# The low parts of g move from VectorE to GpSimd while the second layer's weights are prepared

## The chip, the cores and the metric

The kernel runs on one core of one Trainium2 chip. A core has a matrix engine (TensorE: PE in the views, with its weight loads as PEld), a vector engine (VectorE: DVE), an activation engine (ScalarE: ACT), a general engine (GpSimd: POOL) and a queue that issues transfers (SyncE: SP). Each works through its own instructions in order and waits on semaphores for the others. The metric is the device time of one execution in microseconds (us); lower is better.

## The reference, cut to what is computed

```python
def reference(x, state, moe_w_gate, moe_w1, moe_w2, moe_capacity, moe2_w_in, moe2_w_out):
    a = attention(x, state)                  # 4 x 8 x (512 + 32) x 64, softmax both ways
    t = a.transpose(0, 2, 1, 3).reshape(2176, 512)
    t = moe(t, moe_w_gate, moe_w1, moe_w2, moe_capacity)   # 8 experts, best one per row
    return _moe2_ref(t, moe2_w_in, moe2_w_out)

def _moe2_ref(x, w_in, w_out):               # w_in 512 x 2048, w_out 2048 x 512
    h = x @ w_in
    relu6 = np.clip(h + 3.0, 0.0, 6.0)
    g = h * relu6 / 6.0
    return (g @ w_out).astype(np.float32)
```

The inputs of this last function, the "second layer" here, are 64-bit floats in its weights and 32-bit floats in its rows.

## The kernel before

The first 262 us of the profiled execution are attention and the experts; their result lies as rows in `y_pad`. What the change touches is the second layer that follows. Its rows are taken in seven chunks of 256, and its inner width of 2048 in 16 slices of 128, numbered m. For one slice and one chunk the work is this:

- `mm3` (line 1100) computes 128 columns of h for the 256 rows on TensorE, in twelve matmuls (line 1109): each operand is kept as a high and a low part in a reduced float format (`yTh`, `yTl` of the rows, `wh`, `wl` of the weights), and high by high, high by low and low by high are summed. The eight with `wh` come first, the four with `wl` last. Then ScalarE makes `u` (line 1121), VectorE makes `g` (line 1122, one operand in SBUF and one in PSUM), ScalarE rounds it to the high part `gh` (line 1123), and line 1124 subtracts for the low part `gl`. `u` and `g` have two buffers each, `gh` and `gl` seven.
- `mm4` (line 1127) multiplies `gh` and `gl` by the slice's rows of `w_out`, in six matmuls (line 1132), and adds into two PSUM banks; the third of the six is the first to read `gl`.

The weights are made ready on the way. `vload` (line 921) fetches a slice's 64-bit weights in two loads of 512 KB by SP; `vconv` (line 930) turns each load into 32-bit floats with three VectorE instructions (lines 937, 939, 941), and `advance(NA)` issues the next two of them. `prep(m)` (line 945) has ScalarE round the slice to `wh` (line 955) and GpSimd subtract for `wl` (line 956, 128 x 1024). This is needed once, so it goes on beside the first group of two chunks, `gi == 0`; the five chunks after it find all weights ready.

One step of the first group, for a slice m from 1 to 15, is issued in this order: `mm3(m)` of chunk 0, two conversion instructions, `mm3(m)` of chunk 1, two conversion instructions, `prep(m + 2)`, and then `mm4(m - 1)` of both chunks. So TensorE has 24 matmuls of line 1109 and then 24 of line 1132 in a step. VectorE has in a row: g, gl, two conversions, g, gl, two conversions. ScalarE has u, gh, u, gh, wh. GpSimd has one `wl`, and nothing else until the first results are stored (line 1253). The 51 conversion instructions that are left at slice 1 run out in step 13. The order is the program's own; nothing is rearranged.

After the chunks stands a general loop (lines 1351 to 1367) for inputs that fill an expert unevenly; it doesn't run here, and it calls `mm3` without the new argument.

Of the kernel before, what the change touches and what calls it, by code (L numbers as in the profile page):

```python
# [7 lines left out]
F32 = mybir.dt.float32  # L8
# [4 lines left out]
ALU = mybir.AluOpType  # L13
# [582 lines left out]
def full(ctx, tc, x, state, w_gate, w1, w2, capacity, w_in, w_out, out, dbg=None):  # L596
    nc = tc.nc
    V, A, G, T = nc.vector, nc.scalar, nc.gpsimd, nc.tensor
# [316 lines left out]
    def fetch_c(c):  # L915
        return fetch(lambda t: slice(256 * c + 128 * t, 256 * c + 128 * t + 128), c % 3)
# [28 lines left out]
    def prep(m):  # L945
        v = vt.pop(m).bitcast(F32)
        if m == 0:
            wh = vv.tile([128, 1024], F32R, name="wh0")
            wl = vv.tile([128, 1024], F32R, name="wl0")
        elif m < 3:  # L950
            wh, wl = (rw.tile([128, 1024], F32R, name=f"w{n}{m}", tag="raw0") for n in "hl")
        else:
            wh = vv.tile([128, 1024], F32R, name=f"wh{m}", tag=f"v{m - NV - 1}") if m > NV else mw.tile([128, 1024], F32R, name=f"wh{m}")
            wl = mw.tile([128, 1024], F32R, name=f"wl{m}")
        A.copy(wh, v)  # L955
        (V if m in (0, 2) else G).tensor_tensor(out=wl, in0=v, in1=wh.bitcast(F32), op=ALU.subtract)  # L956
        WM[m] = (wh, wl)
# [3 lines left out]
    def advance(n):  # L961

        while n and nextv[1] < 32:
            if nextv[2] is None:
                while nextv[0] < min(32, nextv[1] + NL2):
                    vload(nextv[0])
                    nextv[0] += 1
                nextv[2] = vconv(nextv[1])
            if next(nextv[2], 0) == 0:
                nextv[1] += 1  # L970
                nextv[2] = None
            n -= 1
# [124 lines left out]

    turn3 = [0]

    def mm3(m, yTh, yTl, early=False):  # L1100
        wh, wl = WM[m]
        turn3[0] ^= 1
        ps = (p3.tile([128, 256], F32, name="p3", tag="3") if turn3[0] else pT.tile([128, 256], F32, name="p3", tag="T"))
        pv = ps.rearrange("p (t j) -> p t j", t=2)
        n = 0
        for ops in (((wh, yTh), (wh, yTl)), ((wl, yTh),)):
            for k in range(4):
                for l, r in ops:
                    T.matmul(pv, l[:, 128 * k:128 * k + 128], r[:, :, 128 * k:128 * k + 128], start=n == 0, stop=n == 11)  # L1109
                    n += 1  # L1110
        if early:
            ug = ew.tile([128, 2, ROW], F32, name="xg", bufs=3)
            u, g = ug[:, 0, 0:256], ug[:, 1, 0:256]
            ghl = mk.tile([128, YR], F32, name="yg").bitcast(F32R)
            gh, gl = ghl[:, 0:256], ghl[:, 256:512]
        else:
            u = mw.tile([128, 256], F32, name="u", bufs=2)
            g = mw.tile([128, 256], F32, name="g", bufs=2)
            gh = mw.tile([128, 256], F32R, name="gh", bufs=NH)
            gl = mw.tile([128, 256], F32R, name="gl", bufs=NH)  # L1120
        A.activation(out=u, in_=ps, func=AF.Relu, bias=b3)  # L1121
        V.scalar_tensor_tensor(out=g, in0=u, scalar=6.0, in1=ps, op0=ALU.min, op1=ALU.mult)  # L1122
        A.copy(gh, g)  # L1123
        V.tensor_tensor(out=gl, in0=g, in1=gh.bitcast(F32), op=ALU.subtract)  # L1124
        return gh, gl

    def mm4(m, gh, gl, po, ts=(0, 1)):
        wh, wl = WM[m]
        for t in ts:
            ls = slice(128 * t, 128 * t + 128)  # L1130
            for i, (l, r) in enumerate(((gh, wh), (gh, wl), (gl, wh))):
                T.matmul(po[t], l[:, ls], r[:, 512:1024], start=m == 0 and i == 0, stop=m == 15 and i == 2)  # L1132

    def accs():
        return [pM.tile([128, 512], F32, name="po", tag="M") for _ in range(2)]
# [23 lines left out]
    ft, pr, pe, pg, pid, pth, py = {}, {}, {}, {}, {}, {}, {}  # L1159
# [16 lines left out]
    for s in range(N0, NF):  # L1176
# [59 lines left out]
        if pend and pend[0][0] == s + 2:  # L1236
            p_begin()
    g0 = mm3(0, *ft[0][0][0:2], True)
    g1 = mm3(0, *ft[1][0][0:2], True)
    po = {c: accs() for c in (0, 1)}  # L1240
    late = (0, (0, 1), {0: g0, 1: g1}, po)
# [5 lines left out]
    def put(po, fid, t):  # L1247
        o = mw.tile([128, DM], F32, name="o", bufs=4)
        if t:
            V.tensor_scalar(out=o, in0=po[t], scalar1=C6, scalar2=None, op0=ALU.mult)  # L1250
        else:
            A.activation(out=o, in_=po[t], func=AF.Copy, scale=C6)  # L1252
        G.indirect_dma_start(out=out, out_offset=bass.IndirectOffsetOnAxis(ap=fid[:, t:t + 1], axis=0), in_=o, in_offset=None,  # L1253
                             bounds_check=B * (S + NS) - 1, oob_is_err=False)

    groups = [(0, 1)] + [(c,) for c in range(2, NCS)]
    for gi, gs in enumerate(groups):
        last = gi + 1 == len(groups)
        if gi:
            po = {}  # L1260
        held = {}
        for m in range(0 if gi else 1, 16):
            if gi == 0 and m in (2, 4, 6):
                r = slice(3 * m - 6, min(3 * m, 17))
                nc.sync.dma_start(out=out.rearrange("(p r) d -> p r d", r=17)[:, r], in_=zt[:, 0:DM].unsqueeze(1).broadcast_to([128, r.stop - r.start, DM]))
            gg = {}
            for c in gs:
                gg[c] = mm3(m, *ft[c][0][0:2])
                if gi == 0:
                    advance(NA)  # L1270
            if gi == 0 and m + 2 < 16:
                prep(m + 2)
            lm, ls, lg, lpo = late
            for c in ls:
                if c == NCS - 1 and lm >= 16 - NH:

                    held[lm] = lg[c]
                    mm4(lm, *lg[c], lpo[c], (0,))
                    continue
                mm4(lm, *lg[c], lpo[c])  # L1280
                if lm == 15:
                    put(lpo[c], ft[c][0][2], 0)
                    put(lpo[c], ft[c][0][2], 1)
            if m == 0:
                for c in gs:
                    po[c] = accs()
            late = (m, gs, gg, po)
            if not last and m >= 10:
                for c in groups[gi + 1]:
                    if m == 10:  # L1290
                        ft[c] = fetch_c(c)
                    if m in (12, 14):
                        ft[c][1](m // 2 - 6)
# [104 lines left out]
```

## Time and profile before

| what | us |
|---|---|
| median of three runs | 594.09 (591.84 to 594.51) |
| the profiled execution | 592.67 |
| its span, first to last instruction | 590.9 |
| steps 3 to 15 of the second layer's first group | 276.77 to 358.52 |

TensorE is busy 95% of the span, VectorE 53%, ScalarE 38%, GpSimd 20%. These are averages over stages with different limits. The page's strip of 40 slices shows the busy share of each engine in tenths; VectorE stands at 5 to 8 between 260 and 350 us and at 3 to 4 after it, while TensorE stands at 9 nearly throughout. The granted TensorE clock is full in all slices of the second layer. A row of a timeline gives the start, the duration, the engine, the line and the operation, and in brackets the idle time before it with what ended it. A duration counts from the moment the instruction has what it waited for by semaphore, so a time in which it then can't proceed is inside it.

### The profile page before, as it was taken

To read this page: it belongs to the slowest core of one execution; us is meant where nothing else is said; L and a number is where in the kernel's file an instruction comes from. 1 tells how busy PE (TensorE), PEld (TensorE's weight loads), DVE (VectorE), ACT (ScalarE), POOL (GpSimd) and SP (SyncE) were. 2 spreads that over 40 slices of the span, in tenths; PEclk is the share of its full clock that TensorE was granted. 3 is DMA by queue.
4 is the path that set the end of the run, shared out by engine and by line. 5 is a ranking of instruction groups with operands and counts; after the bars stand their busy time and mean duration, and the time that the engine had idled before them with its cause. 6 is when DMAs were issued, how large, how long until landed. Compare 5 with 4: busy or idle time off the path is not lost.

```text
span 590.9 us, 10478 instructions
## 1 busy us (share of the span) xinstructions
PE 559.8 (95%) x3974; PEld 483.8 (82%) x3974; DVE 316.0 (53%) x726; ACT 222.1 (38%) x462; POOL 118.8 (20%) x169
## 2 busy tenths in 40 slices
PE   6998899899999999999998989999999999999996
PEld 3655689786968798899987768999999999999995
DVE  5788885364726555366888874234334334234331
ACT  4877631242304150325334334233233333333331
POOL 4436534210600110013334431100001001000001
PEclk9999699799999999999999999999999999999999
DMA  6745612998869783244863411001001001000000
GB/s 140 169 161 174 230 76 59 319 361 297 309 216 391 226 312 109 95 136 129 295 201 109 142 55 53 37 2 55 18 1 55 19 0 55 19 1 18 19 2 29
DMA packets 52201, 75.26 MB, mean 127 GB/s; under 512 B 23121, under 2 KB 31313, under 8 KB 51634
## 3 DMA queue, kind: packets, MB, share of 16 engines
q1 hardware_dynamic: 49634, 67.09, 34.1%
q0 software_dynamic: 2240, 7.38, 3.8%
q8 instruction: 33, 0.54, 0.4%
q14 instruction: 22, 0.18, 0.1%
q10 hardware_dynamic: 272, 0.07, 0.0%
HBM read 70.75 MB, written 16.49 MB: 148 GB/s over the span
## 4 chain that ended last, share of the span: by engine, by line
issue 35%; PE 26%; DVE 11%; DMA 6%; ACT 3%; POOL 1%; POOLq 0%; ACTq 0%; DVEq 0%
PE pm L807 9%; PE pm L796 5%; DMA out_dram<-o,fid 5%; PE p L1109 3%; DVE v L941 3%; PE po L1132 3%; PE pm L1064 2%; PE pm L1084 2%; DVE gl L1124 2%; DVE v L939 2%; DVE v L937 2%; DMA st<-in_moe_w_in_dram 2%; ACT w2h L743 1%; ACT gh L1123 1%; DVE g L1122 1%
## 5 line engine op out<-in xcount | busy, mean ns | idle before, releaser
L1109 PE MATMUL p<-yTh,wh 128*128 128x256 f32 x448 | 110.6, 280 | 0.5 <-ACT wh L955 0.5
L1109 PE MATMUL p<-yTl,wh 128*128 128x256 f32 x448 | 110.5, 280 | 0.0
L1122 DVE SCALAR_TENSOR_TENSOR g<-u,p 128x256 f32<-128x256 f32 x110 | 46.1, 419 | 109.3 <-ACT u L1121 109.3
L1121 ACT ACTIVATE u<-p,b 128x256 f32<-128x256 f32 x110 | 52.1, 474 | 106.8 <-PE p L1109 106.7
L1109 PEld LDWEIGHTS p<-yTh,wh 128*128 128x128 f32 x448 | 84.4, 188 | 4.8 <-ACT wh L955 1.0
L1109 PEld LDWEIGHTS p<-yTl,wh 128*128 128x128 f32 x448 | 84.5, 189 | 3.9
L1132 PE MATMUL po<-wh,gh 128*128 128x512 f32 x220 | 86.8, 394 | 0.8 <-ACT gh L1123 0.6
L1132 PE MATMUL po<-wl,gh 128*128 128x512 f32 x220 | 86.1, 391 | 0.0
L1132 PE MATMUL po<-wh,gl 128*128 128x512 f32 x220 | 86.1, 391 | 0.0
L1124 DVE TENSOR_TENSOR gl<-g,gh 128x256 fp32r<-128x256 f32 x110 | 54.2, 493 | 51.9 <-ACT gh L1123 51.9
L1123 ACT CAST gh<-g 128x256 fp32r<-128x256 f32 x110 | 44.7, 406 | 89.6 <-DVE g L1122 89.6
L1109 PE MATMUL p<-yTh,wl 128*128 128x256 f32 x448 | 71.7, 282 | 5.4 <-POOL wl L956 5.4
L1109 PEld LDWEIGHTS p<-yTh,wl 128*128 128x128 f32 x448 | 60.8, 189 | 6.6 <-POOL wl L956 6.6
L1253 POOL DMA_INDIRECT out_dram<-o,fid x14 | 13.8, 988 | 219.5 <-ACT o L1252 162.2
L956 POOL TENSOR_TENSOR wl<-v,wh 128x1024 fp32r<-128x1024 f32 x14 | 35.3, 2523 | 101.4 <-ACT wh L955 83.3
L1132 PEld LDWEIGHTS po<-wh,gl 128*128 128x128 f32 x220 | 41.3, 188 | 10.0 <-DVE gl L1124 0.8
L1132 PEld LDWEIGHTS po<-wh,gh 128*128 128x128 f32 x220 | 41.4, 188 | 7.4 <-ACT gh L1123 2.4
L796 PE MATMUL pm<-xth,w1h 128*128 128x256 f32 x160 | 46.5, 291 | 0.5 <-ACTq L1156 0.5
L796 PE MATMUL pm<-xtl,w1h 128*128 128x256 f32 x160 | 45.7, 286 | 0.0
L796 PE MATMUL pm<-xth,w1l 128*128 128x256 f32 x160 | 45.6, 285 | 0.0
L1132 PEld LDWEIGHTS po<-wl,gh 128*128 128x128 f32 x220 | 41.4, 188 | 5.1
L807 PE MATMUL pm<-htl,w2h 128*128 128x256 f32 x160 | 44.9, 281 | 0.3 <-DVE htl L799 0.2
(284 smaller groups left out, 985.7 us busy)
## 6 DMA issues: line engine op xcount, KB each, us to landing
raw<-in_moe_w_dram SPq DMA_DIRECT2D x80, 512.0 KB
st<-in_moe_w_in_dram SPq DMA_DIRECT2D x16, 512.0 KB
st<-in_moe_w_out_dram SPq DMA_DIRECT2D x16, 512.0 KB
x_rows<-xrow SPq DMA_DIRECT2D x4, 1072.0 KB
xb<-in_x_dram SPq DMA_DIRECT2D x32, 128.0 KB
yg<-y_pad SPq DMA_DIRECT2D x14, 258.0 KB
out_dram<-zt SPq DMA_DIRECT2D x2, 1536.0 KB
y_pad<-y SPq DMA_DIRECT2D x5, 516.0 KB
```

The lines of the kernel that those rows point to most:

```text
L796: T.matmul(ps[:, j], W1[l][k][:, ls], xT[r][:, k], start=k == 0 and i == 0, stop=k == 3 and i == 2)
L807: T.matmul(ps[:, j], W2[l][k // 2][:, k % 2, ls], hT[k // 2][r][:, k % 2], start=k == 0 and i == 0, stop=k == 7 and i == 2)
L937: V.tensor_scalar(out=t, in0=hi, scalar1=3, scalar2=0x3FFFFFFF, op0=ALU.logical_shift_left, op1=ALU.bitwise_and)
L941: V.scalar_tensor_tensor(out=t, in0=lo, scalar=29, in1=t, op0=ALU.logical_shift_right, op1=ALU.bitwise_or)
L956: (V if m in (0, 2) else G).tensor_tensor(out=wl, in0=v, in1=wh.bitcast(F32), op=ALU.subtract)
L1109: T.matmul(pv, l[:, 128 * k:128 * k + 128], r[:, :, 128 * k:128 * k + 128], start=n == 0, stop=n == 11)
L1121: A.activation(out=u, in_=ps, func=AF.Relu, bias=b3)
L1122: V.scalar_tensor_tensor(out=g, in0=u, scalar=6.0, in1=ps, op0=ALU.min, op1=ALU.mult)
L1123: A.copy(gh, g)
L1124: V.tensor_tensor(out=gl, in0=g, in1=gh.bitcast(F32), op=ALU.subtract)
L1132: T.matmul(po[t], l[:, ls], r[:, 512:1024], start=m == 0 and i == 0, stop=m == 15 and i == 2)
L1253: G.indirect_dma_start(out=out, out_offset=bass.IndirectOffsetOnAxis(ap=fid[:, t:t + 1], axis=0), in_=o, in_offset=None, bounds_check=B * ...
```

## The change

`mm3` gets an argument for the engine that makes `gl`, VectorE unless told otherwise. In the first group, slices 1 to 13 name GpSimd: 26 instructions. Slices 14 and 15, slice 0 (made earlier, line 1238) and the other five chunks stay on VectorE.

```diff
-    def mm3(m, yTh, yTl, early=False):
+    def mm3(m, yTh, yTl, early=False, eng=V):
...
-        V.tensor_tensor(out=gl, in0=g, in1=gh.bitcast(F32), op=ALU.subtract)
+        eng.tensor_tensor(out=gl, in0=g, in1=gh.bitcast(F32), op=ALU.subtract)
...
-                gg[c] = mm3(m, *ft[c][0][0:2])
+                gg[c] = mm3(m, *ft[c][0][0:2], eng=V if gi or m > 13 else G)
```

VectorE's instructions of slice 3 and the start of slice 4, before (the number behind a name is the buffer; g_3853 and g_3879 are slice 3 of chunk 0 and 1, st is a loaded weight and v its conversion):

```order
L1122 SCALAR_TENSOR_TENSOR g_3853<-u_3852,p3_3839 128x256
L1124 TENSOR_TENSOR gl_3855<-g_3853,gh_3854 128x256
L941 SCALAR_TENSOR_TENSOR v8_3756<-st_3728,v8_3756 128x512
L937 TENSOR_SCALAR v9_3863<-st_3754 128x512
L1122 SCALAR_TENSOR_TENSOR g_3879<-u_3878,p3_3865 128x256
L1124 TENSOR_TENSOR gl_3881<-g_3879,gh_3880 128x256
L939 SCALAR_TENSOR_TENSOR v9_3863<-st_3754,v9_3863 128x512
L941 SCALAR_TENSOR_TENSOR v9_3863<-st_3754,v9_3863 128x512
L1122 SCALAR_TENSOR_TENSOR g_3919<-u_3918,p3_3905 128x256
```

The same stretch of VectorE now:

```order
L1122 SCALAR_TENSOR_TENSOR g_3853<-u_3852,p3_3839 128x256
L941 SCALAR_TENSOR_TENSOR v8_3756<-st_3728,v8_3756 128x512
L937 TENSOR_SCALAR v9_3863<-st_3754 128x512
L1122 SCALAR_TENSOR_TENSOR g_3879<-u_3878,p3_3865 128x256
L939 SCALAR_TENSOR_TENSOR v9_3863<-st_3754,v9_3863 128x512
L941 SCALAR_TENSOR_TENSOR v9_3863<-st_3754,v9_3863 128x512
L1122 SCALAR_TENSOR_TENSOR g_3919<-u_3918,p3_3905 128x256
```

The two gl are gone, and a g is followed by conversions at once.

GpSimd's instructions of slices 2 to 4 (gl of two chunks each) with the low weights of slices 3 to 6 (wl3 to wl6), as the difference:

```order
 L956 TENSOR_TENSOR wl3_3759<-v3_2733,wh3_3758 128x1024
+L1124 TENSOR_TENSOR gl_3791<-g_3789,gh_3790 128x256
+L1124 TENSOR_TENSOR gl_3814<-g_3812,gh_3813 128x256
 L956 TENSOR_TENSOR wl4_3824<-v4_2993,wh4_3823 128x1024
+L1124 TENSOR_TENSOR gl_3855<-g_3853,gh_3854 128x256
+L1124 TENSOR_TENSOR gl_3881<-g_3879,gh_3880 128x256
 L956 TENSOR_TENSOR wl5_3889<-v5_3282,wh5_3888 128x1024
+L1124 TENSOR_TENSOR gl_3921<-g_3919,gh_3920 128x256
+L1124 TENSOR_TENSOR gl_3946<-g_3944,gh_3945 128x256
 L956 TENSOR_TENSOR wl6_3957<-v6_3469,wh6_3956 128x1024
```

Between two wl now stand the two gl of the slice in work. TensorE, ScalarE and SP have the same rows as before.

## Rows read from the trace of the kernel before

**Rows 1.** Busy us (instructions) by engine, granted clock, DMA, in two stretches
```profile
298.00:358.00 60.00, 53.32 (x327) 45.45 (x327) 48.46 (x75) 24.20 (x50) 22.78 (x9) 1.00 0.39 125
366.00:422.00 56.00, 56.00 (x362) 50.91 (x361) 18.94 (x46) 19.17 (x43) 4.98 (x5) 1.00 0.10 34
```

**Rows 2.** Waits, 296 to 360 us: waiter, awaited: total us, times, longest
```profile
DVE gl L1124 <- ACT gh L1123: 9.9, 21, 0.5
PEld p L1109 <- POOL wl L956: 6.6, 6, 1.5
```

**Rows 3.** TensorE's timeline: first matmul of steps 3, 7, 15, next stage; two wl matmuls
```profile
276.77 0.28 PE L1109 MATMUL p<-yTh,wh 128*128 128x256 f32 x1
...
277.71 0.63 PE L1109 MATMUL p<-yTh,wl 128*128 128x256 f32 x4
...
298.95 0.28 PE L1109 MATMUL p<-yTh,wh 128*128 128x256 f32 x1
...
300.84 0.73 PE L1109 MATMUL p<-yTh,wl 128*128 128x256 f32 x4 [0.78 <-POOL wl L956]
...
351.38 0.39 PE L1109 MATMUL p<-yTh,wh 128*128 128x256 f32 x1 [0.55 <-ACT wh L955]
...
358.52 0.28 PE L1109 MATMUL p<-yTh,wh 128*128 128x256 f32 x1
```

**Rows 4.** VectorE's timeline, from step 7 to step 10
```profile
306.69 0.41 DVE L1122 SCALAR_TENSOR_TENSOR g<-u,p 128x256 f32<-128x256 f32 x1
...
311.22 2.29 DVE L937 TENSOR_SCALAR v<-st 128x512 int32<-128x512 int32 x1 [0.33 <-DMA st<-in_moe_w_in_dram]
...
317.21 0.42 DVE L937 TENSOR_SCALAR v<-st 128x512 int32<-128x512 int32 x1
317.67 0.69 DVE L939 SCALAR_TENSOR_TENSOR v<-st,v 128x512 int32<-128x512 int32 x1
318.28 0.41 DVE L1122 SCALAR_TENSOR_TENSOR g<-u,p 128x256 f32<-128x256 f32 x1
319.17 1.71 DVE L1124 TENSOR_TENSOR gl<-g,gh 128x256 fp32r<-128x256 f32 x1 [0.47 <-ACT gh L1123]
320.80 0.68 DVE L941 SCALAR_TENSOR_TENSOR v<-st,v 128x512 int32<-128x512 int32 x1
321.40 0.41 DVE L937 TENSOR_SCALAR v<-st 128x512 int32<-128x512 int32 x1
321.73 0.41 DVE L1122 SCALAR_TENSOR_TENSOR g<-u,p 128x256 f32<-128x256 f32 x1
322.61 0.43 DVE L1124 TENSOR_TENSOR gl<-g,gh 128x256 fp32r<-128x256 f32 x1 [0.47 <-ACT gh L1123]
322.96 0.69 DVE L939 SCALAR_TENSOR_TENSOR v<-st,v 128x512 int32<-128x512 int32 x1
323.68 2.88 DVE L941 SCALAR_TENSOR_TENSOR v<-st,v 128x512 int32<-128x512 int32 x1
...
326.48 0.41 DVE L1122 SCALAR_TENSOR_TENSOR g<-u,p 128x256 f32<-128x256 f32 x1
```

**Rows 5.** GpSimd's timeline: wl of slice 3, then three beside Rows 4
```profile
272.15 2.57 POOL L956 TENSOR_TENSOR wl<-v,wh 128x1024 fp32r<-128x1024 f32 x1 [14.97 <-PE po L1132]
...
310.85 2.38 POOL L956 TENSOR_TENSOR wl<-v,wh 128x1024 fp32r<-128x1024 f32 x1 [4.64 <-ACT wh L955]
317.87 2.72 POOL L956 TENSOR_TENSOR wl<-v,wh 128x1024 fp32r<-128x1024 f32 x1 [4.64 <-ACT wh L955]
323.61 2.40 POOL L956 TENSOR_TENSOR wl<-v,wh 128x1024 fp32r<-128x1024 f32 x1 [3.02 <-ACT wh L955]
```

**Rows 6.** The tile wl: ns minimum/median/maximum of its subtraction on either engine
```profile
L956 POOL TENSOR_TENSOR wl<-v,wh x14: 2375/2408/2758, 254.8 to 351.4; 128x1024 fp32r<-128x1024 f32 x14
...
L956 DVE TENSOR_TENSOR wl<-v,wh x2: 1218/1222/1225, 247.7 to 259.7; 128x1024 fp32r<-128x1024 f32 x2
```

**Rows 7.** Other two-input operations of GpSimd, early in the kernel, from its timeline
```profile
12.56 0.20 POOL L196 TENSOR_TENSOR capk<-cf 128x1 f32<-128x1 f32 x1
15.18 1.05 POOL L266 TENSOR_TENSOR R<-R,m 128x512 f32<-128x512 f32 x1 [2.42 <-DVE m L265]
```

## The prediction

> **What bounds the kernel now.** I first compared busy time in two stretches of the second layer [rows 1]. While weights are still being made (298 to 358 us) TensorE starts 327 matmuls in 60 us; in the later stage (366 to 422) it starts 362 in 56 us, always busy. The clock is full in both. So the first stretch loses time that the later one doesn't, and VectorE, busy 48 of 60 us there and 19 of 56 later, is the suspect. The waits of that stretch [rows 2] name who comes late: TensorE's weight loads wait six times for wl, 6.6 us in all. GpSimd, which makes wl, is no bottleneck by busy time (22.8 of 60); it waits for wh, and that stands on ScalarE behind the gh of chunk 1, which waits for g from VectorE.
>
> TensorE's timeline [rows 3] gives the size. From step 3 (276.77) to step 7 (298.95) four steps take 22.18 us, 5.545 each. The first wait is in step 7, at 300.84. From step 3 to the next stage (358.52) there are 13 steps in 81.75 us; at 5.545 they would take 72.09. **9.66 us are lost**, and that is all that the change can win here.
>
> VectorE's timeline [rows 4] shows where they come from. Conversions and g repeat after three steps (twelve conversions, four loads): from the g at 306.69 to the one at 326.48 pass 19.79 us, 6.60 per step, over a us more than TensorE needs. Its parts: six times 0.88 from a g to its gl (318.28 to 319.17, 321.73 to 322.61), of which 0.47 is idle time while ScalarE makes gh; six times 0.35 from a gl to the next start (322.61 to 322.96); twelve conversions in pairs of 1.07 (317.21 to 318.28), 0.93 (320.80 to 321.73) and 1.33 (322.96 to 323.68, and the 0.61 that the pair at 317.67 shows after such an instruction), each pair twice: 6.66. That is 14.04 without disturbance. The rest is three instructions that last far longer than their like: a conversion 2.29 in place of 0.42, a gl 1.71 in place of 0.43, a conversion 2.88 in place of 0.69; 5.34 in all, and 0.33 is a wait for a load. Each lies beside a wl on GpSimd [rows 5] and ends just after it: 313.51 against 313.23, 320.88 against 320.59, 326.56 against 326.01. The g at 318.28 ran at its usual 0.41 inside the wl of 317.87. So conversions and gl stand still while GpSimd subtracts, and g does not; where one is held, it ends up to 0.14 sooner than its whole duration behind the other (320.59 + 0.43 = 321.02 against 320.88).
>
> One law joins the two. The wl of slice 3 is there at 274.72 [rows 5] and wanted at 277.71 [rows 3]: 2.99 us of lead. Each of the twelve steps from 3 to 15 uses up the step's period P on the side of VectorE and GpSimd less 5.545. **Loss = 12 x (P - 5.545) - 2.99, and not below zero.** With P = 6.60 it gives 9.67, against 9.66 measured.
>
> **The change part by part.** *Off VectorE:* in steps 1 to 13 the 26 gl and the idle time before each go, 0.88 + 0.35 less the g itself, which then takes about 0.35 from start to next start, as a gl of that size does. An undisturbed pattern is then 6 x 0.35 + 6.66 = 8.76 us, 2.92 per step in place of 4.68. The gl that was held 1.28 us in the pattern is no longer there to be held.
>
> *On to GpSimd:* 26 subtractions of 128 x 256. The trace has none of this size on that engine. From below, a quarter of the 2.41 for 1024 columns: 0.60 [rows 6]. From above, the 1.05 of a subtraction of 512 columns, whose second operand is repeated [rows 7]. The same engine takes 0.20 for one column; 0.20 and a quarter of the other 2.21 give 0.75. I take 0.75, because wl is the same subtraction in the same formats. GpSimd then works 2.40 + 1.50 = 3.90 us a step, under 5.545, so it has the time. A page gives another price: the Trainium skill (GPSIMD Engine Reference, section 3.1, "Elementwise — side-by-side cycle accounting") has an addition take 1.96 times as long on GpSimd as on VectorE, and with 0.43 here that is an estimate of 0.84; the sum by it comes out 2.2 us longer than mine, and the 2.41 against 1.22 of [rows 6] agree with that ratio.
>
> *What they hold up together:* all conversions and all of GpSimd's subtractions exclude each other, by the three pairs of rows above. In a pattern that is four times 0.42 + 0.69 + 0.69, or 7.20, and three times 3.90, or 11.70: 18.90, **6.30 per step if none overlap**. Each of GpSimd's nine pieces can gain the 0.14 of a handover; with all nine P is 5.88. Not every piece meets a conversion, but those that meet none (beside a g, or in idle time) also cost VectorE nothing. I take P = 6.00, nearer to 5.88, since the row that shows a handover shows its 0.14. Loss 12 x 0.455 - 2.99 = 2.47; **gain 9.66 - 2.47 = 7.2 us**.
>
> *New waits:* the g of a slice now waits on VectorE for the gl two before it on GpSimd, since g has two buffers, and behind it stand two conversions. The gl of chunk 0 stands on GpSimd behind the wl issued a step earlier, and the one of chunk 1 stands ahead of the next wl. A wl needs wh, and wh follows gh of chunk 1 on ScalarE by 1.05 or so, longer than a gl; so gl delays wl little, and the gl behind a wl has at most 2.41 to wait, while mm4 wants it a step later. I cost these at nothing; the cover is that step, 5.5 us less the chain of u, g, gh. Should it fail, that is the slower rival below. *SP's loads* are issued when a conversion frees the buffer, so they come sooner; VectorE waited 0.33 for one in this pattern, and I put them at nothing to 0.3 per pattern, 1.2 us in all, inside the range. GpSimd's stores stand behind all of this and start at 362 as the next chunk allows. TensorE's and ScalarE's work is unchanged.
>
> *Sum:* the profiled execution took 592.67, so 592.67 - 7.2 = 585.5. The median of the runs shown is 594.09, 1.4 above it, and the fastest 0.8 below; I allow 0.5 for that: **586.0**.
>
> **The rivals.**
>
> *All of it is won.* If gl takes 0.60 and handovers hold, P is (7.20 + 3 x 3.60 - 1.26) / 3 = 5.58, the lead of 2.99 covers twelve steps, and the time is 592.67 - 9.66 = 583.0. For it: the nearly idle GpSimd and the lead. Against: the 0.20 that one column costs.
>
> *The exclusion eats half of it.* With no overlap P is 6.30, the loss 6.07 and the time 589.1. For it: conversions come in dependent chains, so a held one delays the next. Against: the handovers read above. The Trainium skill says as much of this change (Perfetto Trace Analysis, "Optimizing Scalar/DVE Operations": offloading between those two engines "might not help", as they share a read port). By that rule this rival would be the likely one; the trace agrees that they exclude each other, but the gap of 0.47 before each gl goes in any case.
>
> *Nothing is won.* A gl of about 1.05 with handovers gives P = (7.20 + 13.50 - 1.26) / 3 = 6.48, loss 8.2, time 591.2; somewhat more holding leads to 592.7. That the change does nothing at all is excluded by the order, which has 26 gl on GpSimd.
>
> *Slower.* If every us of GpSimd holds VectorE, and none falls beside a g or in idle time, P is 2.92 + 2.40 + 2 gl. It decides from P = 6.60 on, which a gl of 0.64 reaches; at 0.90, midway between my value and the upper bound, P is 7.12, the loss 15.9, and the time 592.67 + 6.2 = 598.9. Place: a conversion held by gl, the next g late, its gh late, hence wh, hence wl. For it: three of the three wl in the pattern were met by a held instruction. Against: VectorE, at 2.92 of its own, has idle time in a 5.5 us step in which it can't be held, and a g runs through.
>
> **How the numbers follow.** Forecast 0.53, all won 0.18, half eaten 0.14, nothing 0.08, slower 0.07. Half a per cent is 3.0 us, about what a measurement of this kernel can tell from no change. Half eaten lies at 3.6 gain, so a third of it falls within the bound: faster 0.53 + 0.18 + 0.09 = 0.80, same 0.05 + 0.08 = 0.13, slower 0.07. The range goes from all won, counted from the fastest run (591.84 - 9.66 = 582.2), to the dear gl (591.2): 582.0 to 591.0. It leaves out slower, most of nothing, and a little at the low end.
>
> **What would show it.** Right: gl rows on GpSimd near 0.75; VectorE without line 1124 until step 14 and without the 0.47 gaps; g following its u within a few tenths in chunk 0; steps of TensorE at 5.55 well past step 7, and its waits for wl cut from 6.6 us to under 2.5; the stage after slice 15 starting some 7 us earlier, with everything behind it as before. Wrong: conversions of 2 to 3 us at two or three places in each step; gl of 1 us or more; weight loads waiting for gl (line 1132) or VectorE's g waiting for GpSimd; or the steps just as long with other names in the waits.

## The result, and the profile after

The changed kernel takes 586.56 us (median; 585.12 to 586.87) against 594.30 (591.84 to 594.59) for the kernel before in the same comparison: a ratio of 0.987, 95% interval 0.984 to 0.991, or 7.7 us less. The execution that was profiled took 586.76, with a span of 584.7 against 590.9.

The whole time is a blunt measure here. Step 3 of the second layer started at 276.77 in the profile of before and at 277.81 after. The shift is older than the change: an addition of VectorE well ahead of the first instruction that was moved (line 811) started at 257.31 before and at 258.71 after. In the later experiments, all but the one with the early fills, step 3 started anywhere from 274.35 to 277.86. So the text compares the **stage from step 3 to the first matmul after slice 15**, which has the same 13 steps in every kernel: 81.75 us before, 72.09 at TensorE's own pace of 5.545 a step. (Slices 1 and 2, the first whose gl moves, lie ahead of it; what they gain shows in the stage only as lead.) TensorE's timeline of the changed kernel, the lines that answer to [rows 3] (start, duration, instruction, in brackets the wait and what ended it):

```profile
277.81 0.28 PE L1109 MATMUL p<-yTh,wh 128*128 128x256 f32 x1
...
278.75 0.52 PE L1109 MATMUL p<-yTh,wl 128*128 128x256 f32 x3
...
311.09 0.28 PE L1109 MATMUL p<-yTh,wh 128*128 128x256 f32 x1
...
335.15 0.62 PE L1109 MATMUL p<-yTh,wl 128*128 128x256 f32 x3 [0.20 <-POOL wl L956]
...
347.67 0.73 PE L1109 MATMUL p<-yTh,wl 128*128 128x256 f32 x4 [0.66 <-POOL wl L956]
...
352.40 0.28 PE L1109 MATMUL p<-yTh,wh 128*128 128x256 f32 x1
```

The stage takes 352.40 - 277.81 = 74.59 us, **7.16 less than before, with 2.50 of the 9.66 still lost**. Six steps, 3 to 8, take 33.28 to 311.09, 5.547 each, where before step 7 was already late; the excess begins in step 10 and is largest in the last three. The waits of the whole stage, 277.81 to 352.40, which answer to [rows 2] (waiter, awaited: total us, times, longest):

```profile
DVE g L1122 <- ACT u L1121: 7.5, 7, 1.9
DVE v L937 <- DMA st<-in_moe_w_in_dram: 3.9, 2, 3.4
DVE v L937 <- DMA st<-in_moe_w_out_dram: 3.2, 3, 1.5
DVE gl L1124 <- ACT gh L1123: 1.9, 4, 0.5
PEld p L1109 <- POOL wl L956: 1.6, 4, 0.9
```

TensorE's weight loads waited 6.6 us for wl before and wait 1.6 now. VectorE now waits for u at times, that is for TensorE, which is what an engine off the path does. Waits for loads have grown: 0.8 us in the stage before, 7.1 now, 3.4 of them at once. VectorE's timeline, to be laid beside [rows 4]:

```profile
304.51 0.66 DVE L937 TENSOR_SCALAR v<-st 128x512 int32<-128x512 int32 x1 [1.42 <-DMA st<-in_moe_w_out_dram]
305.21 1.11 DVE L939 SCALAR_TENSOR_TENSOR v<-st,v 128x512 int32<-128x512 int32 x1
306.24 0.41 DVE L1122 SCALAR_TENSOR_TENSOR g<-u,p 128x256 f32<-128x256 f32 x1
306.57 0.68 DVE L941 SCALAR_TENSOR_TENSOR v<-st,v 128x512 int32<-128x512 int32 x1
310.64 0.43 DVE L937 TENSOR_SCALAR v<-st 128x512 int32<-128x512 int32 x1 [3.39 <-DMA st<-in_moe_w_in_dram]
310.98 0.41 DVE L1122 SCALAR_TENSOR_TENSOR g<-u,p 128x256 f32<-128x256 f32 x1
311.31 0.69 DVE L939 SCALAR_TENSOR_TENSOR v<-st,v 128x512 int32<-128x512 int32 x1
312.03 1.17 DVE L941 SCALAR_TENSOR_TENSOR v<-st,v 128x512 int32<-128x512 int32 x1
...
313.90 0.69 DVE L939 SCALAR_TENSOR_TENSOR v<-st,v 128x512 int32<-128x512 int32 x1
...
315.74 2.37 DVE L941 SCALAR_TENSOR_TENSOR v<-st,v 128x512 int32<-128x512 int32 x1
```

And GpSimd's, beside [rows 5]:

```profile
302.28 2.61 POOL L956 TENSOR_TENSOR wl<-v,wh 128x1024 fp32r<-128x1024 f32 x1 [0.20 <-ACT wh L955]
304.85 0.92 POOL L1124 TENSOR_TENSOR gl<-g,gh 128x256 fp32r<-128x256 f32 x1
307.17 0.74 POOL L1124 TENSOR_TENSOR gl<-g,gh 128x256 fp32r<-128x256 f32 x1 [1.40 <-ACT gh L1123]
308.11 2.40 POOL L956 TENSOR_TENSOR wl<-v,wh 128x1024 fp32r<-128x1024 f32 x1 [0.20 <-ACT wh L955]
311.91 0.74 POOL L1124 TENSOR_TENSOR gl<-g,gh 128x256 fp32r<-128x256 f32 x1 [1.40 <-ACT gh L1123]
314.05 1.14 POOL L1124 TENSOR_TENSOR gl<-g,gh 128x256 fp32r<-128x256 f32 x1 [1.40 <-ACT gh L1123]
315.15 2.40 POOL L956 TENSOR_TENSOR wl<-v,wh 128x1024 fp32r<-128x1024 f32 x1
```

Where no load is late, a g is followed by a conversion within 0.34 us; the gap is gone. The two engines still exclude each other, both ways: the conversion at 305.21 ends at 306.32, held by the gl that ends at 305.77; the gl at 314.05 takes 1.14 instead of 0.74, held by the conversion at 313.90. The conversion at 315.74 lasts 2.37, until the wl beside it is through. The tile gl on GpSimd (ns minimum/median/maximum):

```profile
L1124 POOL TENSOR_TENSOR gl<-g,gh x26: 737/919/1198, 270.3 to 343.7; 128x256 fp32r<-128x256 f32 x26
```

Free, it takes 0.74; the median of 0.92 has the holding in it, and twelve of the 26 last 1 us or more. SP's timeline shows where the late load comes from (line 925 loads weights, line 1265 fills the output with zeros):

```profile
300.02 0.43 SPq L1265 DMA_DIRECT2D out_dram<-zt  x1
302.65 0.37 SPq L925 DMA_DIRECT2D st<-in_moe_w_in_dram  x1
```

The load went out 2.6 us behind a fill of 1280 KB and was waited for until 310.64, 8.0 us later.

### The profile page after: what moved, and what is told of

Same layout as the page of the kernel before. It is cut to its first block, busy times and chain, and to the rows that moved or that the text cites. A ratio compares the mean times of both kernels' runs of the same rounds, so it can differ in the third digit from the quotient of the medians.

```text
span 584.7 us, 10490 instructions
## 1 busy us (share of the span) xinstructions
PE 558.1 (95%) x3974; PEld 483.9 (83%) x3974; DVE 307.7 (53%) x700; ACT 222.1 (38%) x462; POOL 142.5 (24%) x195
## 4 chain that ended last, share of the span: by engine, by line
issue 37%; PE 21%; DMA 11%; DVE 8%; ACT 3%; POOL 0%; POOLq 0%; ACTq 0%; DVEq 0%
PE pm L807 9%; DMA out_dram<-o,fid 6%; PE pm L796 5%; PE pm L1084 2%; DMA st<-in_moe_w_out_dram 2%; DVE v L941 2%; PE pm L1064 2%; PE p L1109 2%; DVE v L939 1%; DMA st<-in_moe_w_in_dram 1%; DVE v L937 1%; ACT w2h L743 1%; DMA raw<-in_moe_w_dram 1%; DVE g L1122 1%; PE po L1132 1%
## 5 line engine op out<-in xcount | busy, mean ns | idle before, releaser
L1124 DVE TENSOR_TENSOR gl<-g,gh 128x256 fp32r<-128x256 f32 x84 | 36.7, 437 | 39.8 <-ACT gh L1123 39.8
L807 PE MATMUL pm<-hth,w2h 128*128 128x256 f32 x160 | 45.0, 281 | 0.3 <-issue 0.2
```

The lines of the kernel that those rows point to most:

```text
L807: T.matmul(ps[:, j], W2[l][k // 2][:, k % 2, ls], hT[k // 2][r][:, k % 2], start=k == 0 and i == 0, stop=k == 7 and i == 2)
L1124: eng.tensor_tensor(out=gl, in0=g, in1=gh.bitcast(F32), op=ALU.subtract)
```

## The experiments

My theory was the one of the prediction: the gap ahead of gl is what the change removes, and GpSimd's work costs VectorE time because the two exclude each other. Its rival is the plain reading of the change: VectorE had too much to do, and 26 x 0.43 us of work left it. Each number of a stage is the time from the first matmul of step 3 to the first one after slice 15, in the one execution of that kernel that was profiled; the two profiles of the changed kernel differ by 0.17 us. The order is that of the argument, not of the runs.

| kernel | median us | ratio to before (95%) | stage, from and to | stage us | lost over 72.09 |
|---|---|---|---|---|---|
| before | 592.8 to 594.3 in three comparisons | 1 | 276.77 to 358.52 | 81.75 | 9.66 |
| changed | 586.56 | 0.987 (0.984 to 0.991) | 277.81 to 352.40 | 74.59 | 2.50 |
| changed, again | 584.60 | 0.986 (0.982 to 0.990) | 277.38 to 351.80 | 74.42 | 2.33 |
| gl late on VectorE | 582.74 | 0.983 (0.980 to 0.987) | 274.35 to 346.98 | 72.63 | 0.54 |
| gl late and wl, all on VectorE | 582.32 | 0.981 (0.977 to 0.984) | 277.86 to 349.82 | 71.96 | none |
| changed, wl on VectorE | 582.42 | 0.983 (0.979 to 0.986) | 276.67 to 348.63 | 71.96 | none |
| changed, fills early | 585.59 | 0.986 (0.984 to 0.989) | 279.85 to 353.02 | 73.17 | 1.08 |
| changed, gl of chunk 0 twice | 587.86 | 0.991 (0.988 to 0.994) | 276.34 to 353.05 | 76.71 | 4.62 |
| half of the change | 589.03 | 0.994 (0.992 to 0.996) | 275.56 to 354.09 | 78.53 | 6.44 |
| changed, gap put back | 604.86 | 1.021 (1.017 to 1.025) | 275.30 to 370.84 | 95.54 | 23.45 |

### The gap without the move, and the move without the gap

The first diff is against the kernel before.

```diff
-        V.tensor_tensor(out=gl, in0=g, in1=gh.bitcast(F32), op=ALU.subtract)
+        def low():
+            V.tensor_tensor(out=gl, in0=g, in1=gh.bitcast(F32), op=ALU.subtract)
...
+        later.append(low)
...
                 if gi == 0:
                     advance(NA)
+                    rest[0]()
```

> The kernel before, with one change of order: in the first group VectorE makes gl itself, but after the two conversions instead of ahead of them, so the 0.47 us in which it waited for gh is filled. GpSimd does wl alone. If the gap and the mutual exclusion explain the time: VectorE's own step is 2.92 + 2 x 0.35 = 3.62 us, the exclusive work 7.20 + 7.20 + 2.58 = 16.98 us in three steps or 5.66 a step, less 0.14 for handovers: P about 5.5 and no loss, or 6.0 and a loss of 2.7 if every wl holds VectorE throughout. So 7.0 to 9.7 us below the kernel before, as fast as the changed kernel or up to 2.5 us faster. If it is the 26 x 0.43 = 11 us of work leaving VectorE that counts, this stays within 2 us of the kernel before.

VectorE keeps all its work, and the stage takes 72.63 us: 9.12 less than before, 2 less than with GpSimd's help. A piece of VectorE's timeline of this kernel:

```profile
313.53 0.41 DVE L937 TENSOR_SCALAR v<-st 128x512 int32<-128x512 int32 x1
313.86 0.41 DVE L1125 TENSOR_TENSOR gl<-g,gh 128x256 fp32r<-128x256 f32 x1
314.20 0.41 DVE L1122 SCALAR_TENSOR_TENSOR g<-u,p 128x256 f32<-128x256 f32 x1
314.53 0.68 DVE L939 SCALAR_TENSOR_TENSOR v<-st,v 128x512 int32<-128x512 int32 x1
315.24 0.69 DVE L941 SCALAR_TENSOR_TENSOR v<-st,v 128x512 int32<-128x512 int32 x1
315.85 0.42 DVE L1125 TENSOR_TENSOR gl<-g,gh 128x256 fp32r<-128x256 f32 x1
316.40 0.42 DVE L1122 SCALAR_TENSOR_TENSOR g<-u,p 128x256 f32<-128x256 f32 x1
```

From a g to its gl pass 1.65 us, filled with two conversions, and gl starts without a wait (four waits for gh are left, in the steps without conversions). The rival wanted this kernel within 2 us of before; it is 10 us below it.

The counterpart leaves gl on GpSimd and has VectorE wait for gh all the same:

```diff
         eng.tensor_tensor(out=gl, in0=g, in1=gh.bitcast(F32), op=ALU.subtract)
+        if eng is G:
+            V.tensor_copy(u[:, 0:1], gh[:, 0:1].bitcast(F32))
```

> The changed kernel, with VectorE made to wait for gh again: it copies one column of gh in the place where gl stood in steps 1 to 13, about 0.15 us each. gl stays on GpSimd. If the idle gap ahead of gl was what cost: VectorE's own step rises from 2.92 by 2 x 0.6 to about 4.1 us, with some 2 to 2.9 us of holding by GpSimd P is 6.1 to 7.0, so steps 3 to 15 take 76 to 87 us, most or all of the gain lost. If the 26 x 0.43 us of work taken off VectorE is what counts: within 1 us of the changed kernel's 74.6.

The stage takes 95.54 us, more than my upper end of 87, and the kernel is 2% slower than before: all of the work is off VectorE, and in the stage the gain of 7.16 has turned into a loss of 13.8 against before. VectorE and GpSimd in this kernel:

```profile
321.07 0.41 DVE L1122 SCALAR_TENSOR_TENSOR g<-u,p 128x256 f32<-128x256 f32 x1
321.96 0.15 DVE L1126 COPY u<-gh 128x1 f32<-128x1 f32 x1 [0.47 <-ACT gh L1123]
322.03 1.00 DVE L937 TENSOR_SCALAR v<-st 128x512 int32<-128x512 int32 x1
323.06 2.84 DVE L939 SCALAR_TENSOR_TENSOR v<-st,v 128x512 int32<-128x512 int32 x1
```
```profile
322.00 0.74 POOL L1124 TENSOR_TENSOR gl<-g,gh 128x256 fp32r<-128x256 f32 x1 [2.12 <-ACT gh L1123]
322.96 2.40 POOL L956 TENSOR_TENSOR wl<-v,wh 128x1024 fp32r<-128x1024 f32 x1 [0.21 <-ACT wh L955]
```

The wait of 0.47 is back, and when it ends, GpSimd has just started: the copy and gl wait for the same gh, so the conversion at 322.03 is held by gl (1.00 in place of 0.42) and the next one by wl (2.84 in place of 0.69). Most steps take 7.2 to 7.5 us. The two experiments together decide between the theory and its rival: with the gap closed the work can stay on VectorE, and with the gap kept the move wins nothing. **The gap had to go, and the move was only a way to be rid of it.**

What the gap costs by itself is not shown, since each run also changes how long the two engines hold each other up. Call an instruction of VectorE held for as long as it lasts beyond the shortest of its like. Summed over its timeline in the stage that is some 20 us before, 21 in the changed kernel, 14 with gl late, and 37 with the gap put back. Before and with the gap put back VectorE waits equally long for gh (12.8 us); so what makes the last kernel slower than before is mostly holding, and not the gap alone.

### What GpSimd's help costs

```diff
-        (V if m in (0, 2) else G).tensor_tensor(out=wl, in0=v, in1=wh.bitcast(F32), op=ALU.subtract)
+        V.tensor_tensor(out=wl, in0=v, in1=wh.bitcast(F32), op=ALU.subtract)
```

The diff is against the kernel with gl late on VectorE.

> As the run with gl late on VectorE, and VectorE makes all wl too (1.22 us each by its two rows of before), so GpSimd does nothing in this stage. If exclusion makes GpSimd's help costly: P = (2.10 + 2.10 + 6.66 + 3 x 1.14) / 3 = 4.8 us, under TensorE's 5.545, no loss, 9.7 us below the kernel before and about 2 us below the changed one; no conversion longer than 0.7 us. If VectorE needs relief: its step comes over 5.55, and the run is slower than the one with gl late alone.

The stage takes 71.96 us, TensorE's own pace, and no weight load of TensorE waits for wl. VectorE now does everything; its timeline:

```profile
316.52 0.68 DVE L939 SCALAR_TENSOR_TENSOR v<-st,v 128x512 int32<-128x512 int32 x1
317.24 0.69 DVE L941 SCALAR_TENSOR_TENSOR v<-st,v 128x512 int32<-128x512 int32 x1
317.86 0.42 DVE L1125 TENSOR_TENSOR gl<-g,gh 128x256 fp32r<-128x256 f32 x1
318.19 1.22 DVE L956 TENSOR_TENSOR wl<-v,wh 128x1024 fp32r<-128x1024 f32 x1
319.32 0.41 DVE L1122 SCALAR_TENSOR_TENSOR g<-u,p 128x256 f32<-128x256 f32 x1
```

Nothing is held in the stage: each instruction lasts what its like do, and wl costs VectorE 1.22, where beside GpSimd a single conversion could stand for 2.2 us longer than its own time. The same on the changed kernel, with GpSimd left with gl alone:

```diff
-        (V if m in (0, 2) else G).tensor_tensor(out=wl, in0=v, in1=wh.bitcast(F32), op=ALU.subtract)
+        (V if m in (0, 2) or m > 3 else G).tensor_tensor(out=wl, in0=v, in1=wh.bitcast(F32), op=ALU.subtract)
```

> The changed kernel with wl of slices 4 to 15 on VectorE as well (1.22 us there for 2.41 on GpSimd), so that GpSimd makes only gl. If exclusion with GpSimd's long subtraction is what is left of the loss: VectorE's own step is 2.92 + 1.14 = 4.06 us, held by at most 1.5: P up to 5.56, steps 3 to 15 within 0.7 us of 72.1 despite the late load. If VectorE's load is what matters: P rises by 1.14 over the changed kernel's 5.9 to 7.0, and the steps take over 80 us.

71.96 us as well. Giving VectorE 1.22 us more to do in each step from slice 4 on made the stage 2.6 us shorter. Its instructions are held 7 us in place of 21. So what was left of the loss hung on wl being made by GpSimd, and a late load did no harm here: VectorE still waited 7.5 us for loads in this run, up to 3.5 at once. The run does not show that exclusion is the whole of it. A wl that takes 1.22 us in place of 2.41 is also there sooner, which adds 1.2 us to the lead once, about half of the 2.5 that were lost.

### Half of the change

```diff
-                gg[c] = mm3(m, *ft[c][0][0:2], eng=V if gi or m > 13 else G)
+                gg[c] = mm3(m, *ft[c][0][0:2], eng=V if gi or m > 13 or c else G)
```

> Half of the change: GpSimd makes gl of chunk 0 in steps 1 to 13, VectorE that of chunk 1. VectorE's own step is 2.92 + 0.88 = 3.80 us, with one gap in place of two. With P midway between the 6.60 of before and the 5.88 of the changed kernel's steps 5 to 9, 6.24, the loss is 12 x 0.695 - 3 = 5.3: steps 3 to 15 take 77.4 us, half of the gain. If one gap is short enough for the lead to cover, they take 74 or less; if the order on GpSimd matters (a gl behind wl), over 79.

78.53 us against the 77.4 expected: 3.2 of the 7.2 us gained with half of the gaps gone. The gain goes about with the number of gaps. It goes with the work moved as well, so this run doesn't tell the theory from its rival.

### More work on GpSimd

```diff
         eng.tensor_tensor(out=gl, in0=g, in1=gh.bitcast(F32), op=ALU.subtract)
+        if twice:
+            eng.tensor_tensor(out=gl, in0=g, in1=gh.bitcast(F32), op=ALU.subtract)
...
-                gg[c] = mm3(m, *ft[c][0][0:2], eng=V if gi or m > 13 else G)
+                gg[c] = mm3(m, *ft[c][0][0:2], eng=V if gi or m > 13 else G, twice=gi == 0 and m <= 13 and c == 0)
```

> The changed kernel with the gl of chunk 0 made twice on GpSimd in steps 1 to 13, the same values both times: 13 x 0.74 us more work there. If loss = 12 x (P - 5.545) - 3 holds and the step is bound by exclusion: P = 6.04 + 0.74 = 6.78, loss 11.8, so 9.3 us above the changed kernel and about 1.6 above the kernel before. If GpSimd's idle time (5.5 - 3.9 a step) takes it up: within 1 us of the changed kernel.

This one missed. The stage takes 76.71 us, 2.1 more than the changed kernel, where the law with my sum wanted 9.3 and the rival at most 1. Thirteen more subtractions (line 1126) beside the 26:

```profile
L1124 POOL TENSOR_TENSOR gl<-g,gh x26: 729/902/1198, 268.4 to 345.0; 128x256 fp32r<-128x256 f32 x26
L1126 POOL TENSOR_TENSOR gl<-g,gh x13: 799/1054/1075, 269.6 to 344.0; 128x256 fp32r<-128x256 f32 x13
```

From the end of wl of slice 5 to that of slice 9, ahead of the late load in both kernels, a step of GpSimd is 6.19 us here and 5.88 in the changed kernel: 0.31 more for 0.80 of work. So of a us that GpSimd works more, some 0.4 reach the step. Over all twelve steps P is 6.18 against 6.04 in the changed kernel, and the lead 3.33; with these the law gives a loss of 4.3, and 4.6 is measured. So the tie between P and the loss held, and the sum that was to give P did not.

VectorE's timeline shows where most of the difference went. The eleven extra pieces that fall in the stage are 8.8 us. Its instructions are held 29 us, against 21 and 23 in the two profiles of the changed kernel, so most of the added work did hold VectorE. But its waits for u and for loads shrink to 8.6 us, from 14.6 and 12.3: much of the holding fell into time in which VectorE would have waited anyway.

### The late load

```diff
-            if gi == 0 and m in (2, 4, 6):
-                r = slice(3 * m - 6, min(3 * m, 17))
-                nc.sync.dma_start(out=out.rearrange("(p r) d -> p r d", r=17)[:, r], in_=zt[:, 0:DM].unsqueeze(1).broadcast_to([128, r.stop - r.start, DM]))
...
     def early():
         nc.sync.dma_start(out=x_rows[0:1, :], in_=zt[0:1, 248:248 + ROW])
+        for a in (0, 6, 12):
+            r = slice(a, min(a + 6, 17))
+            nc.sync.dma_start(out=out.rearrange("(p r) d -> p r d", r=17)[:, r], in_=zt[:, 0:DM].unsqueeze(1).broadcast_to([128, r.stop - r.start, DM]))
```

> The changed kernel with the three zero fills of the output issued in the attention part instead of in steps 2, 4 and 6. In the changed kernel a load issued at 302.65 behind the third fill was waited for until 310.64, and VectorE waited 7.1 us for loads in the stage. If that wait sets the remaining loss of 2.5 us: the waits go, and the run is 1 to 2.5 us below the changed kernel. If the lead covers it: within 0.7 us of the changed kernel. If the fills cost elsewhere: above it, with a longer time before 262 us.

VectorE has no wait for a load in the stage any more, and the stage takes 73.17 us, 1.4 less than the changed kernel. So the waits account for about 1.0 to 1.4 of the 2.5 us that were left: this execution entered step 3 with a lead of 4.04 us in place of 3.64, and those 0.4 us may be part of the 1.4. The kernel as a whole gained no time that shows (585.59, ratio 0.986): step 3 started at 279.85, 2.0 us later than in any run with the fills in their old place. It may be that the fills, issued at 30 us, cost elsewhere what they save here; that rests on one profile, and what they would delay there was not followed up.

### The changed kernel again

> The changed kernel as it is, for comparison on this chip. Steps 3 to 15 should again take about 74.6 us, 2.5 over 72.1, with VectorE waiting some 7 us for loads, most of it behind the third zero fill. If the wait for the load was an accident of one execution, the steps take under 74.

There is no edit. The stage takes 74.42 us, and VectorE waited 5.6 us for loads, so the late load belongs to the kernel and not to one execution.

## Why the prediction was right, step by step

The forecast was 586.0 us, the time is 586.56; it wanted 7.2 us from the stage, and 7.16 came. Point by point:

- **Where the time was lost: right.** The loss was all in the stage, and the stretch behind it is unchanged (232.4 us to the end before, 232.3 after). The gap of 0.47 with the 0.35 of gl behind it is what left VectorE, and the experiments show that of the two the gap had to go, while gl could have stayed.
- **The price of gl on GpSimd: right.** 0.75 was taken, 0.74 is its time when it isn't held. The quarter of the long subtraction (0.60) and the 512-column one (1.05) are not it; the estimate from the ratio in the Trainium skill (GPSIMD Engine Reference, section 3.1), 0.84, was further off than the one from the rows. "gl of 1 us or more" was listed as a sign of being wrong, and twelve of 26 are that long; they are held by conversions, and a sum of exclusive work has that time in it, whoever holds whom.
- **P = 6.00: right in size, by errors that cancel.** The wl of slices 3 and 15 end at 275.11 and 347.62, which is 6.04 a step. The lead was larger too: wl of slice 3 was there at 275.11 and wanted at 278.75, 3.64 instead of 2.99. With these two the law gives 12 x 0.497 - 3.64 = 2.3, against 2.47 in the forecast and 2.50 measured. That the two errors, some half a us each, cancel is luck, and so is part of the 6.04: it isn't made as I had it. From slice 5 to slice 9 the step is 5.88 (their wl end at 287.00 and 310.51, 23.51 us for four), which was my lower bound, and with 5.88 throughout the law would give 0.4. What comes on top is in good part a term that I had put at nothing to 0.3 a pattern: *SP's loads*. A conversion that is done sooner frees its buffer sooner, but a load behind a 1280 KB fill lands 8.0 us after its issue all the same. VectorE waited 7.1 us for loads, and the run with the fills early puts their cost at 1.0 to 1.4. Even the 5.88 has some such waits in it; without any, in that run, the same four steps take 5.80 each.
- **The law: right as bookkeeping.** With the P and the lead of its own profile it comes within about 0.3 us of the loss for every kernel that loses time, but for the one with the gap put back (21.7 against 23.45). It says that the loss is a lead used up by a longer step; it doesn't say what makes the step long.
- **What the last 1.08 us are** is only argued: they fall in steps 14 and 15. In step 12 a subtraction of VectorE for the next chunk's rows (line 911) stands 2.67 us beside a wl, 0.69 otherwise, and the gh of step 13, the last wh and the last wl come after it. No run took it away.
- **New waits at nothing: right** in the changed kernel. Weight loads of TensorE waited 0.4 us for gl, once, and VectorE's g did not wait for GpSimd.
- **The sum of exclusive work as a law for P: wrong as a slope.** It met the changed kernel by my choice of how many handovers count, and it failed where GpSimd's work was changed by itself: 6.78 expected, 6.18 measured. What failed there is the assumption that added work of GpSimd lengthens the step in full: much of it went into time in which VectorE waited anyway.
- **The rivals.** "All of it is won" is what the kernels with wl on VectorE do, by a way that I hadn't considered. "Slower" is what the kernel with the gap put back does: a held conversion, a late g, a late gh, wh and wl, at 7.2 to 7.5 us a step. So its mechanism is real, and in the changed kernel it didn't decide. "Half of it" and "nothing" wanted steps of 6.30 and 6.48. The rule of the Trainium skill (Perfetto Trace Analysis, "Optimizing Scalar/DVE Operations") that moving work between these two engines might not help names a real cost: the two exclude each other in every trace in which GpSimd subtracts in this stage (a conversion of 2.37 us in place of 0.69). Whether the move helps hung on the gap here: 1.3% less time with the gap gone, 2.1% more with it kept.

The best kernels here are those that keep wl on VectorE: 582.3 to 582.4, 10.4 to 10.5 us (1.7 to 2.0%) below the kernel before in the same comparison. In whole time their intervals overlap that of the changed kernel measured again, and the kernel with gl late alone (582.74) can't be told from them; in the stage they are 2.6 us shorter than the changed kernel.

## What to carry to other kernels

Before work is moved off an engine that sets the pace, see how much of its step is work and how much is waiting within its order: here an instruction that needed a result just sent to another engine stood first in line, and putting two independent instructions ahead of it gained more than taking it away. Work for GpSimd that reads two tensors is not free for VectorE; count the time in which the two exclude each other, and ask whether VectorE would do the same in half of it. And compare kernels by the stage that a change touches, from one fixed instruction to another, when whole times of one kernel vary by a third of the effect (591.84 to 594.59 for an effect of 7.7 us).

## What the hardware showed that was not expected

The exclusion works both ways and with an overlap: a held gl on GpSimd takes up to 1.20 us for 0.74, a held conversion ends up to 0.14 us sooner than its whole duration after the holder. And a single two-input subtraction of 128 x 1024 costs this pair of engines less on VectorE (1.22 us, with nothing held where GpSimd has no work) than on GpSimd (2.41 us, in which VectorE can do little but g).
